# ZW with n2 innermost: contiguous 32x32 transposes, stepped copies and a stepped stationary operand

## The chip, the cores and the metric

The kernel runs on 1 core of one Trainium2 chip. The metric is device time in microseconds (us) of one execution. An execution's program uses TensorE (PE; its weight loads are listed apart as PEld), VectorE (DVE), ScalarE (ACT), GpSimd (POOL) and the DMA queues, of which SyncE's (SP) carries most loads and stores here.

## The reference

`x` has shape 8 x 3072 x 256. The first half is a convolution over the sequence by Fourier transform, the second a mixture of 8 experts with a top-1 gate and a capacity of 768 tokens per expert:

```python
X = np.fft.rfft(x, axis=1)
Y = X * (filt_r + 1j * filt_i)[None]
y = np.fft.irfft(Y, n=3072, axis=1).reshape(-1, 256)
logits = y @ w_gate                      # 256 -> 8
# token i goes to its best expert while that one has fewer than 768 tokens
h = np.maximum(einsum('ecd,edf->ecf', disp, w1), 0)     # 256 -> 1024
out = gate * einsum('ecf,efd->ecd', h, w2)              # 1024 -> 256, 0 for other tokens
```

## The kernel before

Since the experts are full after some 6144 tokens, only the first `NB0` = 3 batches (0, 1 and 2) are transformed if every expert fills up on them, which is so with these inputs. Their convolutions take the first part of the span, the experts the rest, which runs on TensorE almost without a gap.

The sequence is split as n = 32*n1 + n2 (96 x 32). For one batch and both halves `h` of 128 channels the steps are:

- `a` (L226; in batch 0 `a_half`, L217): matmuls over n1 with the table `A` as stationary operand; a bank of 512 values per partition is copied by ACT to `ZW`, a tile of 128 partitions x 2 halves x 32 (n2) x 128 (channels). One call of `a` handles 4 values of n2 in two banks, 8 calls make a batch.
- `t` (L235): four DVE instructions per batch, each of which transposes 64 of 128 channels of one half in blocks of 32 partitions x 32 values of n2, in place in `ZW`. q = 0, 1 are half 0, q = 2, 3 are half 1.
- `bm` (L239): four matmuls with `self.ZW[:, h, p, :]` (128 x 128) as stationary and the constant `Bc` as moving operand, into one bank. Each f32 matmul is two weight loads and two matmuls in the trace, so a call of `bm` is x8 there. A batch has 12 calls, 6 groups `g` by 2 halves.
- `b` (L247): DVE multiplies the bank by the filter (two instructions, L259), POOL adds and subtracts (L263, L264). `g` (L267) transposes the result back with matmuls (L276) and splits it in a high and a low part on ACT and DVE; `bi` (L283) is the inner transform back (L290), copied by ACT to `V`.
- `ti` (L335) transposes `V` as `t` does `ZW`; `V` has 144 or 128 channels innermost. `ai` (L340) is the last stage back (L349), copied by ACT to `rt` and stored by DMA.

`middle` runs `b`, `g` and `bi` in an order written out by hand: b(0,0), b(0,1), b(1,0), b(1,1), g(0), and so on; up to two steps of the `ai` of the batch before (`ahead`) are put between the first `b`s. All queues are in program order. Batch 0 computes `bm` of half 0 for all six groups right after its second half's `a_half`. For batches 1 and 2 the order is: four `ti` of the batch before, beside `a` of the new one; then the `ai` steps beside four `t`; then `middle`. In batch 2 the routing of the batch before (one-hot rows on DVE, L452 to L454, and their matmuls L462) is interleaved with these. The matmuls of L462 have operands `ol[:, :, i]` and `oh[:, :, :, i]` in f16, both with a step of 8 elements (16 bytes) between neighbours, 128 stationary columns and 96 moving ones. L430 is a DVE reduction that reads f32 with a step of 32 elements (128 bytes), L394 one of the same size that reads neighbours.

Of the kernel before, what the change touches and what calls it, by code (L numbers as in the profile page):

```python
# [9 lines left out]
F32 = mybir.dt.float32  # L10
# [6 lines left out]

# The sequence is split as n = 32*n1 + n2 (96 x 32), its frequencies as
# k = k1 + 96*k2.  Complex rows of k1 come in pairs (2 per group of 128
# partitions), a partition is (j, c, p or n2 or slot): j the member of the pair,  # L20
# c real or imaginary, p the group.
N1, N2, NP = 96, 32, 24
CH = 272  # channels of the transform back: y[0:128], 8 + 8 halves of the logits, y[128:256]
HS = ((0, 144), (144, 128))  # its two blocks: start and size

# [53 lines left out]
def fftconv_moe_kernel(ctx, tc, x, fr, fi, fny, wg, w1, w2, ca, cai, cb, out, cap):  # L79
    nc = tc.nc  # L80
    NB, SEQ, D = x.shape[0], N1 * N2, 256
    E, FF = w1.shape[0], w1.shape[2]
    NT = (cap + 127) // 128          # slot tiles of an expert
    NSLOT = E * NT                   # slot tiles in all
    NTOK = NB * SEQ
    NB0 = min(NB, -(-E * cap // SEQ) + 1)
    NF = FF // 128
    NE = min(3, NT)                  # slot tiles of the first expert that go ahead of the last batch
    assert 3 <= NB0 < NB
# [25 lines left out]
    def row_of_slot(idx, n):  # L115
        # tacc holds the token of a slot plus 1, 0 where the slot is empty
        nc.vector.tensor_scalar(out=idx, in0=tacc[:, :n], scalar1=-1.0, scalar2=0.0, op0=ALU.add, op1=ALU.max)
# [11 lines left out]
    def interleave(*lists):  # L129
        # merges the lists of steps evenly  # L130
        marks = sorted(((i + 1) / (len(l) + 1), j, i) for j, l in enumerate(lists) for i in range(len(l)))
        for _, j, i in marks:
            lists[j][i]()

    HOLD = 2  # steps of the last but one batch's transform back that run ahead of the last batch's

# [4 lines left out]
    class Conv:  # L141
        """The convolution of one batch, in steps."""

        def __init__(self, base, top, side, resident):
            self.base, self.wk, self.side, self.resident = base, top, side, resident
            self.ZW = top.tile([128, 2, N2, 128], F32, name="ZW", bufs=1)
            self.Bc = top.tile([128, 4, 128], F32, name="Bc", bufs=1)
            self.BIh = top.tile([128, 2, 128], F32R, name="BIh", bufs=1)
            self.BIl = top.tile([128, 2, 128], F32R, name="BIl", bufs=1)
            self.IG = top.tile([128, 2, 136], F32, name="IG", bufs=1)  # [1 | gate] and [gate | 1]  # L150
            self.FNY = top.tile([128, 2], F32, name="FNY", bufs=1)
            if resident:
                self.A = side.tile([N1, N2, 128], F32, name="A", bufs=1)
                self.F = [top.tile([128, 2, QS], F32, name=n, bufs=1) for n in ("FRT", "FIT")]
            self.xts, self.Fs, self.Ac, self.dropped, self.ysb, self.ycs, self.bps = {}, {}, {}, False, {}, {}, {}
# [15 lines left out]
        def drop_dc(self, t, col):  # L171
            # the transform back ignores the imaginary part of the constant term
            for h in range(2):
                nc.vector.memset(t[:, h, col:col + 1], 0.0)
# [42 lines left out]
        def a_half(self, h, c):  # L217
            xt = self.xts.pop((h, c))
            for k in range(2):
                ps = bank()  # L220
                for i in range(4):
                    nc.tensor.matmul(ps[:, i * 128:(i + 1) * 128], self.Ac[c * 2 + k][:, i, :], xt[:, k * 4 + i, :], start=True, stop=True)
                n2 = c * 8 + k * 4
                nc.scalar.copy(self.ZW[:, h, n2:n2 + 4, :], ps.rearrange("p (t d) -> p t d", d=128))  # L224

        def a(self, c):  # L226
            xt, A = self.xts.pop(c), self.Ac[c]
            for h in range(2):
                ps = bank()
                for i in range(2):  # L230
                    nc.tensor.matmul(ps[:, i * D:(i + 1) * D], A[:, h * 2 + i, :], xt[:, h * 2 + i, :], start=True, stop=True)
                n2 = c * 4 + h * 2
                nc.scalar.copy(self.ZW[:, :, n2:n2 + 2, :].rearrange("p h t d -> p t h d"), ps.rearrange("p (t h d) -> p t h d", h=2, d=128))

        def t(self, q):  # L235
            v = self.ZW[:, q // 2, :, q % 2 * 64:q % 2 * 64 + 64].rearrange("p t d -> p d t")
            nc.vector.transpose(v, v)  # L237

        def bm(self, g, h):  # L239
            ps = bank()  # L240
            for i in range(4):
                p = g * 4 + i
                nc.tensor.matmul(ps[:, i * 128:(i + 1) * 128], self.ZW[:, h, p, :],  # L243
                                 self.Bc[:, 1 if p == NP - 1 else 0, :], start=True, stop=True)
            return ps
# [48 lines left out]
        def middle(self, V, fill, first=(), last=()):  # L294
            """Steps from the transformed rows to the rows of the transform back."""
            fill, first = list(fill), list(first)
# [43 lines left out]
    def ai(V, dst, h, L=None, eng=None):  # L340
        """Steps of the last stage of the transform back, one bank of rows each."""
        c0, w = HS[h]
        k = 512 // w
# [28 lines left out]
    def route(L, last, ohp):  # L372
        """Slots of a batch's tokens: steps up to the slot, then the table of the slots' tokens."""
        t = lambda nm, sh, dt=F32: p1b.tile(sh, dt, name=nm, tag=nm, bufs=1)
# [47 lines left out]
        def f9():  # L422
            # es: 128 * NT * expert
            st["es"] = t("es", [N1, N2])
            V_.tensor_scalar(out=st["es"], in0=st["m2"][:, 0, :], scalar1=float(-128 * NT), scalar2=float(128 * NT * E),
                             op0=ALU.mult, op1=ALU.add)
# [51 lines left out]

# [1 line left out]
    W, X, Gt, H = {}, {}, {}, {}  # L480
# [8 lines left out]
    def turn(rows, n, pool, spare=False):  # L489
        """The rows' transposes in two parts; spare leaves the Vector engine alone."""  # L490
        xh = pool.tile([128, 2, n * 128], F32R, name="xh", tag="xh")
        xl = pool.tile([128, 2, n * 128], F32R, name="xl", tag="xl")
        for h in range(2):
            ps = bank()
            for i in range(n):
                nc.tensor.transpose(ps[:, i * 128:(i + 1) * 128], rows[:, i, h * 144:h * 144 + 128], ident)  # L496
            split(xh[:, h, :], xl[:, h, :], ps[:, :n * 128], pool if spare else None)
        return xh, xl
# [29 lines left out]

# [1 line left out]
    base_ctx, v_ctx, top_ctx, side_ctx, raw_ctx = (ExitStack() for _ in range(5))  # L530
# [19 lines left out]
    def routing_constants():  # L550
# [13 lines left out]
        io(nv[:, 0, :], [[1, N2]], -SEQ // 2, N2)  # L564
        # tri[p, m] = 1 where p < m
        nc.gpsimd.affine_select(out=tri, in_=ones, pattern=[[1, N1]], compare_op=ALU.is_gt, fill=0.0,
                                base=0, channel_multiplier=-1)

    def early_count():
        # reaches the capacity where the first expert's early slots are all taken  # L570
        nc.vector.tensor_tensor(out=tot[:, E:E + 1], in0=tot[:, 0:1], in1=lack, op=ALU.add)

    def full_flag():
        # the least number of tokens an expert has got, and the count of the early slots
        ps = bank()
# [7 lines left out]
    def load_w(e, raw, pool):  # L583
        """Steps that load an expert's weights and split them."""
        loads, splits, ws = [], [], []
# [22 lines left out]
    with tc.manual_schedule():  # L608
        # batches that are needed whatever the routing
        V = new_V(vp)  # L610
        order = [(h, c) for h in range(2) for c in range(4)]
        for i, (h, c) in enumerate(order):
            # the rows of V in front of its padding are free until the transform back
            dst = V[c // 3][:N1, c % 3 * 8:c % 3 * 8 + 8, 0:128] if h else None
# [10 lines left out]
        nc.vector.memset(zt, 0.0)  # L625
        # the tensor engine warms up while the first loads are under way
        ps = bank()
# [42 lines left out]

        # the last of them: its route goes on beside the last stage of the transform back
        b = NB0 - 1
# [58 lines left out]

        # the other batches only while an expert still has room
        least = nc.values_load(flag[0:1, 0:1], min_val=0, max_val=NTOK)
        with tc.If(least < cap):  # L734
            with ExitStack() as gp:
# [8 lines left out]
                with tc.For_i(NB0, NB, 1) as b:  # L744
# [14 lines left out]
                    for f in S1 + S2:  # L759
                        run(f)  # L760
                # the rows of the slots move to ybuf in slot order
                row_of_slot(idxg, NSLOT)
# [144 lines left out]
```

## Time and profile before

| | |
|---|---|
| median of 3 runs | 561.33 us (559.0 to 561.54) |
| profiled execution, span from first to last instruction | 557.8 us |
| granted TensorE clock, mean over the span | 0.945 of full |
| PE busy | 507.6 us (91%) |
| DVE, ACT, POOL busy | 315.5, 239.3, 241.5 us |
| the four stages `t` on DVE: 12 instructions | 50.3 us |

The profiled execution's own time is not listed beside its span; the runs' median lies 3.5 us above that span, the lowest run 1.2 us. Times inside the profile are counted from the first instruction. Busy times of PE overlap each other (matmuls are pipelined), so what a stretch costs is read from the starts of successive instructions.

### The profile page before, as it was taken

To read this page: it belongs to the slowest core of one execution; us is meant where nothing else is said; L and a number is where in the kernel's file an instruction comes from. 1 tells how busy PE (TensorE), PEld (TensorE's weight loads), DVE (VectorE), ACT (ScalarE), POOL (GpSimd) and SP (SyncE) were. 2 spreads that over 40 slices of the span, in tenths; PEclk is the share of its full clock that TensorE was granted. 3 is DMA by queue.
4 is the path that set the end of the run, shared out by engine and by line. 5 is a ranking of instruction groups with operands and counts; after the bars stand their busy time and mean duration, and the time that the engine had idled before them with its cause. 6 is when DMAs were issued, how large, how long until landed. Compare 5 with 4: busy or idle time off the path is not lost. (4 is left out here: it accounts for less than half of the span.)

```text
span 557.8 us, 9332 instructions
## 1 busy us (share of the span) xinstructions
PE 507.6 (91%) x3564; PEld 492.7 (88%) x3564; DVE 315.5 (57%) x531; ACT 239.3 (43%) x563; POOL 241.5 (43%) x245
## 2 busy tenths in 40 slices
PE   6789999699994998978889999999999999999992
PEld 5778989699894898976879999999999999999992
DVE  0587799787998889997134533334333353333500
ACT  3404766146640355472063633536335363363410
POOL 4016301363031650342674666836667366673021
PEclk9978999799996999888779999999999999999997
DMA  9999347990449905550430506016050160511000
GB/s 220 274 359 407 155 114 199 337 397 27 114 119 327 326 1 181 156 156 8 152 120 32 208 29 217 32 49 212 29 212 32 51 214 29 180 60 49 11 29 28
DMA packets 58420, 81.64 MB, mean 146 GB/s; under 512 B 4096, under 2 KB 37376, under 8 KB 58240
## 3 DMA queue, kind: packets, MB, share of 16 engines
q1 hardware_dynamic: 43264, 51.20, 28.9%
q10 hardware_dynamic: 10496, 16.78, 9.0%
q0 software_dynamic: 4608, 12.98, 6.5%
q8 instruction: 31, 0.51, 0.4%
q14 instruction: 21, 0.17, 0.1%
HBM read 39.46 MB, written 41.48 MB: 145 GB/s over the span
## 5 line engine op out<-in xcount | busy, mean ns | idle before, releaser
L508 DVE SCALAR_TENSOR_TENSOR hl<-ps,hh 128x384 fp32r<-128x384 f32 x124 | 67.3, 556 | 98.1 <-ACT hh L502 86.5
L826 PE MATMUL ps<-wbh,hh 128*128 128x256 f32 x384 | 109.5, 285 | 4.4 <-DVEq L734 4.4
L826 PE MATMUL ps<-wbh,hl 128*128 128x256 f32 x384 | 108.4, 282 | 0.1
L826 PE MATMUL ps<-wbl,hh 128*128 128x256 f32 x384 | 108.5, 282 | 0.0
L524 PE MATMUL ps<-xh,wah 128*128 128x384 f32 x256 | 87.8, 343 | 2.4 <-issue 1.7
L524 PE MATMUL ps<-xl,wah 128*128 128x384 f32 x256 | 87.6, 342 | 0.2 <-issue 0.2
L524 PE MATMUL ps<-xh,wal 128*128 128x384 f32 x256 | 87.4, 342 | 0.0
L830 POOL DMA_INDIRECT y<-ob,idxs x48 | 47.6, 991 | 88.7 <-ACT ob L829 85.3
L502 ACT ACTIVATE hh<-ps 128x384 fp32r<-128x384 f32 x128 | 61.7, 497 | 54.3 <-PE ps L524 48.3
L826 PEld LDWEIGHTS ps<-wbh,hh 128*128 128x128 f32 x384 | 73.6, 192 | 4.7 <-issue 4.7
L826 PEld LDWEIGHTS ps<-wbl,hh 128*128 128x128 f32 x384 | 73.7, 192 | 0.0
L826 PEld LDWEIGHTS ps<-wbh,hl 128*128 128x128 f32 x384 | 73.5, 191 | 0.2 <-issue 0.2
L263 POOL TENSOR_TENSOR t<-t,t 128x256 f32<-128x256 f32 x33 | 24.5, 742 | 86.0 <-DVE t L259 75.2
L237 DVE STREAM_TRANSPOSE ZW<-ZW 128x2048 f32<-128x2048 f32 x12 | 50.3, 4240 | 19.0 <-ACT ZW L224 19.0
L829 ACT ACTIVATE ob<-ps,gt 128x256 f32<-128x256 f32 x48 | 22.7, 472 | 89.0 <-PE ps L826 61.4
L243 PE MATMUL ps<-Bc,ZW 128*128 128x128 f32 x288 | 42.7, 307 | 16.0 <-DVE ZW L237 15.8
L485 POOL DMA_INDIRECT rows<-ybuf,idxg x45 | 45.4, 1009 | 26.9 <-DVEq L734 13.5
L243 PEld LDWEIGHTS ps<-Bc,ZW 128*128 128x128 f32 x288 | 40.4, 222 | 17.0 <-issue 16.0
L349 PE MATMUL ps<-V,AI 128*96 128x144 f32 (+1 forms) x384 | 50.9, 294 | 4.4 <-ACT rt L351 2.8
L338 DVE STREAM_TRANSPOSE V<-V 128x2304 f32<-128x2304 f32 (+1 forms) x12 | 50.7, 4260 | 5.5 <-ACT V L292 5.5
L349 PEld LDWEIGHTS ps<-V,AI 128*96 128x96 f32 x384 | 49.1, 174 | 5.3 <-ACT rt L351 3.0
L351 ACT COPY rt<-ps 96x432 f32<-96x432 f32 (+2 forms) x57 | 30.0, 541 | 52.2 <-PE ps L349 43.1
(123 smaller groups left out, 907.1 us busy)
## 6 DMA issues: line engine op xcount, KB each, us to landing
y<-zt SPq DMA_DIRECT2D x12, 2048.0 KB
raw<-w ACTq DMA_DIRECT2D x16, 1024.0 KB
xt<-x SPq DMA_DIRECT2D x16, 384.0 KB
ybuf<-rt SPq DMA_DIRECT2D x30, 162.0 KB
ybuf<-rt SPq DMA_DIRECT2D x24, 192.0 KB
A<-ca SPq DMA_DIRECT2D x8, 192.0 KB
xt<-x SPq DMA_DIRECT2D x8, 192.0 KB
V<-x SPq DMA_DIRECT2D x8, 192.0 KB
```

What stands on the lines that cost most here:

```text
L237: nc.vector.transpose(v, v)
L243: nc.tensor.matmul(ps[:, i * 128:(i + 1) * 128], self.ZW[:, h, p, :], self.Bc[:, 1 if p == NP - 1 else 0, :], start=True, stop=True)
L263: eng.tensor_tensor(out=t1[:, :, 0, :], in0=t1[:, :, 0, :], in1=t2[:, :, 1, :], op=ALU.subtract)
L338: nc.vector.transpose(v, v)
L349: nc.tensor.matmul(ps[:N1, i * w:(i + 1) * w], AI[:, n0 + i, :], V[h][:, n0 + i, :], start=True, stop=True)
L351: nc.scalar.copy(rt[:, :n * w], ps[:N1, :n * w])
L485: nc.gpsimd.indirect_dma_start(out=rows[:, t, :], out_offset=None, in_=yrows[:lim, :], in_offset=bass.IndirectOffsetOnAxis(ap=idx[:, j + t ...
L502: nc.scalar.activation(out=hi, in_=ps, func=f)
L508: nc.vector.scalar_tensor_tensor(out=lo, in0=ps, scalar=0.0, in1=hi.bitcast(F32), op0=ALU.max, op1=ALU.subtract)
L524: nc.tensor.matmul(ps[:, :n * 128], w[:, kk, m * 128:(m + 1) * 128], y[:, kk, o], start=k == 0, stop=k == 5)
L826: nc.tensor.matmul(ps[:, :D], y[:, m, o], w[:, m, :], start=m == 0 and j == 0, stop=m == NF - 1 and j == 2)
L830: ins = nc.gpsimd.indirect_dma_start(out=out, out_offset=bass.IndirectOffsetOnAxis(ap=idxs[:, j:j + 1], axis=0), in_=ob, in_offset=None, b ...
```

## The change

`ZW` becomes 128 partitions x 2 halves x 128 channels x 32 (n2). The four transposes of a batch then read and write 2048 neighbouring values of a partition in order. The copies out of PSUM write 4 neighbouring values, then step 128 bytes; to do so they read the bank with a step of 128 values (512 bytes). `a` is cut so that one bank holds one half and four values of n2, as `a_half` had it: 4 matmuls of 128 moving columns for a bank in place of 2 of 256. The stationary operand of `bm` has a step of 32 values (128 bytes) between its columns.

```diff
-            self.ZW = top.tile([128, 2, N2, 128], F32, name="ZW", bufs=1)
+            self.ZW = top.tile([128, 2, 128, N2], F32, name="ZW", bufs=1)
...
-                nc.scalar.copy(self.ZW[:, h, n2:n2 + 4, :], ps.rearrange("p (t d) -> p t d", d=128))
+                nc.scalar.copy(self.ZW[:, h, :, n2:n2 + 4], ps.rearrange("p (t d) -> p d t", d=128))
...
-                for i in range(2):
-                    nc.tensor.matmul(ps[:, i * D:(i + 1) * D], A[:, h * 2 + i, :], xt[:, h * 2 + i, :], start=True, stop=True)
-                n2 = c * 4 + h * 2
-                nc.scalar.copy(self.ZW[:, :, n2:n2 + 2, :].rearrange("p h t d -> p t h d"), ps.rearrange("p (t h d) -> p t h d", h=2, d=128))
+                for i in range(4):
+                    nc.tensor.matmul(ps[:, i * 128:(i + 1) * 128], A[:, i, :], xt[:, i, h * 128:(h + 1) * 128], start=True, stop=True)
+                nc.scalar.copy(self.ZW[:, h, :, c * 4:c * 4 + 4], ps.rearrange("p (t d) -> p d t", d=128))
...
-            v = self.ZW[:, q // 2, :, q % 2 * 64:q % 2 * 64 + 64].rearrange("p t d -> p d t")
+            v = self.ZW[:, q // 2, q % 2 * 64:q % 2 * 64 + 64, :]
             nc.vector.transpose(v, v)
...
-                nc.tensor.matmul(ps[:, i * 128:(i + 1) * 128], self.ZW[:, h, p, :],
+                nc.tensor.matmul(ps[:, i * 128:(i + 1) * 128], self.ZW[:, h, :, p],
```

## Rows read from the trace of the kernel before

**Rows 1.** First line of the page.

```profile
span 557.8 us, 9332 instructions
```

**Rows 2.** Waits of PE, 0 to 214 us: total us, times, longest.

```profile
PE ps L243 <- DVE ZW L237: 15.8, 4, 7.5
...
PE ps L276 <- POOL t L264: 2.0, 4, 0.8
...
PE pr L408 <- DVE cs L404: 1.2, 2, 0.8
```

**Rows 3.** Timeline of DVE, batch 0 to 1: start us, us, instruction.

```profile
69.33 16.43 DVE L338 STREAM_TRANSPOSE V<-V 128x2304 f32<-128x2304 f32 x4 [2.59 <-ACT V L292]
85.68 16.55 DVE L237 STREAM_TRANSPOSE ZW<-ZW 128x2048 f32<-128x2048 f32 x4
```

**Rows 4.** Timeline of PE, batch 0 to 1.

```profile
68.82 13.98 PE L231 MATMUL ps<-xt,A 96*128 96x256 f32 x64
...
95.72 1.06 PE L243 MATMUL ps<-Bc,ZW 128*128 128x128 f32 x8
102.37 2.05 PE L243 MATMUL ps<-Bc,ZW 128*128 128x128 f32 x8 [5.60 <-DVE ZW L237]
...
108.31 1.06 PE L243 MATMUL ps<-Bc,ZW 128*128 128x128 f32 x8
...
138.41 8.80 PE L231 MATMUL ps<-xt,A 96*128 96x256 f32 x40
```

**Rows 5.** Timeline of PE, batch 0.

```profile
28.66 7.18 PE L243 MATMUL ps<-Bc,ZW 128*128 128x128 f32 x48
38.04 3.20 PE L243 MATMUL ps<-Bc,ZW 128*128 128x128 f32 x16 [2.19 <-DVE ZW L237]
...
44.54 1.65 PE L243 MATMUL ps<-Bc,ZW 128*128 128x128 f32 x8
```

**Rows 6.** Timelines of DVE and of PE, batch 1 to 2.

```profile
173.00 4.14 DVE L237 STREAM_TRANSPOSE ZW<-ZW 128x2048 f32<-128x2048 f32 x1
...
168.62 1.13 PE L243 MATMUL ps<-Bc,ZW 128*128 128x128 f32 x8 [0.47 <-DVE ZW L237]
177.28 2.05 PE L243 MATMUL ps<-Bc,ZW 128*128 128x128 f32 x8 [7.54 <-DVE ZW L237]
...
183.33 1.56 PE L276 MATMUL ps<-IG,t 128*128 128x136 f32 x12
```

**Rows 7.** DVE's groups of instructions, shapes apart, 0 to 270 us: busy, mean ns.

```profile
L237 DVE STREAM_TRANSPOSE ZW<-ZW 128x2048 f32<-128x2048 f32 x12 | 50.3, 4240 | 19.0 <-ACT ZW L224 19.0
L280 DVE TENSOR_TENSOR yl<-ps,yh 128x408 fp32r<-128x408 f32 x48 | 26.5, 575 | 5.9 <-ACT yh L279 4.6
...
L338 DVE STREAM_TRANSPOSE V<-V 128x2304 f32<-128x2304 f32 x6 | 25.0, 4194 | 5.5 <-ACT V L292 5.5
...
L430 DVE TENSOR_REDUCE s<-cs 96x32 f32<-96x256 f32 x3 | 1.8, 603 | 0.0
...
L394 DVE TENSOR_REDUCE m<-sc 96x32 f32<-96x256 f32 x3 | 1.2, 416 | 0.1
```

**Rows 8.** Timeline of PE's weight loads at two places.

```profile
110.48 1.87 PEld L243 LDWEIGHTS ps<-Bc,ZW 128*128 128x128 f32 x16
112.27 1.46 PEld L276 LDWEIGHTS ps<-IG,t 128*128 128x128 f32 x12
...
155.72 1.31 PEld L462 LDWEIGHTS <-ol 96*128 96x128 f16 x8
157.07 3.05 PEld L349 LDWEIGHTS ps<-V,AI 128*96 128x96 f32 x24
```

**Rows 9.** Instructions on tile ZW: ns min/median/max, first and last start.

```profile
L233 ACT COPY ZW<-ps x32: 586/586/590, 69.9 to 153.8; 128x512 f32<-128x512 f32 x32
```

**Rows 10.** Windows of batch 1's middle: length, busy by engine, granted clock, DMA.

```profile
102.40:109.20 6.80, 6.80 (x40) 6.80 (x41) 3.82 (x7) 1.16 (x2) 2.81 (x4) 0.65 1.04 383
109.20:138.40 29.20, 28.44 (x238) 27.87 (x237) 24.84 (x53) 16.11 (x61) 15.92 (x22) 1.00 0.62 235
```

## The prediction

> **What bounds the kernel now.** I read the list of PE's waits first, then the timelines of PE and DVE around each wait, then the groups by duration. The span is 557.8 us [rows 1], the median 561.33, so 3.5 us lie outside the span; the sum is made on the span and added to the median. Every step of the change lies before 214 us. After that the experts run in an order that no edit touches, so a delay or gain before 214 us moves the end by as much. Up to there the reader is to see one large wait [rows 2]: PE waits 15.8 us, in four pieces, for the transposes of `ZW`; the next causes are 2.0 us (POOL) and 1.2 us (the routing's scan). So PE is the bound nearly everywhere, and DVE only where a batch's eight transposes stand in a row.
>
> The three places: in batch 0 PE has done half 0's six `bm` calls (x48) and waits 2.19 us until 38.04 [rows 5]. Between batches 0 and 1 DVE works without a break from 69.33, four `ti` and then four `t` of 16.55 us together [rows 3]; PE finishes `ai` and bm(0,0) at 96.8 and waits until 102.37, 5.60 us [rows 4]. Between batches 1 and 2 it waits 7.54 us until 177.28 [rows 6]. [...]
>
> **The transposes.** Twelve at 4.24 us each [rows 7]. What does contiguous access make of them? `V`'s transposes move 2304 values in 4.19 us, less time than 2048 values of `ZW` take [rows 7]; the step between values is 576 bytes there and 512 here. So the time goes by the access pattern, not only by the count. Two reductions of 256 values differ in their step alone: 603 ns with 128 bytes (L430), 416 ns without (L394) [rows 7], so a step costs (603 - 416)/256 = 0.73 ns per value. Without a step the rate is (575 - 416)/(408 - 256) = 1.05 ns per value (L280 against L394), by which 2048 values take 0.416 + 1792 x 1.05 ns = 2.3 us. Bounds: 2.3 to 4.24 us (nothing gained). I take 2.3, since the stepped reduction comes to 1.05 + 0.73 = 1.78 ns per value, close to the transpose's 4240/2048 = 2.07. A batch's four save 7.8 us of DVE.
>
> **A's copies.** Now 586 ns for 512 values [rows 9]. No row has a stepped read of PSUM or a stepped write of ACT. Below: nothing, 0.59 us. Above: DVE's 0.73 ns per value, once for the read, once more for the write, 0.59 + 0.37 + 0.37 = 1.33 us. I take one of the two, 0.96, since the write keeps runs of four. That is hidden: the first copy starts at 69.9 [rows 9], sixteen at 0.96 end at 85.3, and `t` does not start before 85.68, behind `ti` [rows 3]. The cover is gone from (85.68 - 69.9)/16 = 0.99 us on.
>
> **A's matmuls.** 64 matmuls of 256 columns take 13.98 us [rows 4]; now they are 128 of 128 columns, each with a weight load. A pair of this size starts every (112.27 - 110.48)/16 = 0.112 us [rows 8], so 14.3 us: +0.4 us in batches 1 and 2.
>
> **B's stationary operand.** This decides. A weight load of 128 columns and its matmul take 0.112 us now, 0.9 us per call of `bm`. The only matmuls with stepped operands are L462's, and they start every (157.07 - 155.72)/8 = 0.169 us [rows 8], although they are f16 and stream only 96 columns. If the moving operand set that pace, it took 0.169/96 = 1.76 ns per stepped value, DVE's 1.78 again; a load of 128 stepped columns at this rate takes 0.22 us and can no longer hide behind its matmul. If the stationary operand set it, a stepped column costs 0.169/128 = 1.32 ns, and a pair of `bm` 0.169 us. If neither carries over to f32, 0.112 us stays. Bounds: 0.112 to 0.225 us a pair. I take 0.22, because two engines agree on that price for a value that is read with a step. Then a `bm` call takes 1.76 us, 0.86 us more, and PE, the bound, pays this.
>
> [...]
>
> **The sum, place by place.** Batch 0: from 28.66 to 41.24 PE runs 64 pairs and the wait [rows 5]; 64 x 0.22 us end at 42.7, so +1.5, and the wait is swallowed. The 3.3 us up to bm(2,1) at 44.54 ran at the low clock (8 pairs in 1.65 us there); without idle time before them I take 0.9 us back. Three later calls cost 0.86 each, +2.6; bm(2,1) itself +0.1; of the small waits on ACT and POOL 0.7 us disappear behind the slower PE. Together +2.6.
>
> Batch 1: `t` ends at 85.7 + 4 x 2.3 = 94.9, so PE no longer waits. It reaches bm(0,0) at 95.72 + 0.4 = 96.1; four `bm` calls and two `ai` steps between them (8 pairs, 0.9 us each) end at 96.1 + 7.0 + 1.8 = 104.9, against 109.2 (108.31 and 0.9) [rows 4]: -4.3. The other eight calls cost +6.9, of which the 0.8 us of waits on POOL and the scan in this middle absorb as much. Together +1.8.
>
> Batch 2: DVE's last transpose ends at 177.1 - 7.8 = 169.3 [rows 6]. PE starts bm(0,0) at 168.2 + 0.4 = 168.6 (its wait of 0.47 goes); four calls and one `ai` step end at 168.6 + 7.0 + 0.9 = 176.5, against 183.33 [rows 6]: -6.8. Then +6.9, less about 1.5 of the 2.0 us of waits there. Together -1.4.
>
> Sum: +2.6 + 1.8 - 1.4 = +3.0 us: 560.8 us of span, 561.33 + 3.0 = 564.3 us by the median. The 15.8 us of waiting, and the low clock behind it, are traded for 36 slower `bm` calls. A measurement of this kernel tells about 0.5% (2.8 us) from no change, so this is slower by barely that much.
>
> **Rivals.** *The stationary operand takes its step for free* (pairs stay at 0.112 us). For it: L462's loads read 128 stepped columns in 0.169 us at most, so that stream is not at 1.76 ns there. Against it: they are f16, with a 16-byte step. Batch 0 gains the wait and the low clock, 3.0; batch 1 has four `bm` and two `ai` from 96.1 to 101.5, 7.7 earlier; in batch 2 bm(0,1) starts at 169.4 and bm(1,1) ends at 173.0, 10.3 earlier. Together -21.0: 540.3 us, faster. Between it and the forecast lies the pair of 0.169 us (1.35 us a call): -2, -3.1 and -6.3, 550 us. The sign turns at about 0.21 us a pair.
>
> [...]
>
> *ACT becomes late.* With both prices, 1.33 us a copy, batch 1's last copy ends at 69.9 + 21.3 = 91.2, the last transpose at about 99, and the `ai` copies queue behind on ACT and hold PE's banks. I count 2.5 us in batch 1 and 2 in batch 2 on top of the forecast: 569 us. It decides from 0.99 us a copy on.
>
> *The transposes do not get faster* (the block order, not the memory, sets 2 ns per value). Then the waits stay, and 0.86 us is paid on each call outside them and outside the low clock: about +2.6, +7 and +6.5: 577 us. `V`'s 4.19 us for more values speaks against it.
>
> **Numbers.** Chances: forecast 0.52 (559 to 570 with 0.20 to 0.225 us a pair and 2.3 to 2.6 us a transpose), free stationary operand 0.21, the pair in between 0.12, ACT late 0.09, transposes unchanged 0.06. The range 539 to 571 leaves out the last case and the tails. Faster: 0.21 + 0.12 + 0.05 of the forecast's = 0.38; same (558.5 to 564.1): 0.23 of the forecast's; slower: 0.24 + 0.09 + 0.06 = 0.39. The forecast's own part sits astride the bound, so the three are near each other; 564 stands because it is the likeliest single case.
>
> **What would show it.** In the profile after: the mean of L237 (2.3 us expected); the mean of A's copies on ACT (0.96); the distance between starts of L243's weight loads in a run of eight (0.22); PE's wait for `ZW` gone from the list; the granted clock near 1.00 behind bm(0,0) of batches 1 and 2. Wrong it is if L243's pairs still start every 0.11 us (then 540), or if L237 stays at 4.2. What I can't bound: whether slower pairs, which leave PE's array idle for half of each, let the granted clock fall in batch 0's run of 64; that would cost some more us.

## The result, and the profile after

Measured side by side, the kernel after takes 564.8 us (median of 20 runs, 561.57 to 568.32), the kernel before 562.62 us (20 runs, 556.42 to 565.79): a ratio of 1.0053 with an interval of 1.0029 to 1.0078. (The ratio is not the quotient of the two medians, which is 1.0039.) The forecast was 564 us (564.3 by its sum), or +3.0 us. The profiled execution took 562.22 us with a span of 560.4 us, 2.6 us above that of before [rows 1].

First the page of the kernel after: span and busy times.

```profile
span 560.4 us, 9588 instructions
...
PE 529.5 (94%) x3692; PEld 520.4 (93%) x3692; DVE 294.3 (53%) x531; ACT 238.7 (43%) x563; POOL 240.6 (43%) x245
```

DVE's busy time fell by 21.2 us and PE's rose by 21.9 us. The edit removes one line, so `bm` is now L242, `t` L236 and the copy of `a` L232. The view of the tile `ZW` in the kernel after (ns min/median/max, first and last start):

```profile
L242 PEld LDWEIGHTS ps<-Bc,ZW x288: 292/313/333, 28.8 to 207.0; 128*128 128x128 f32 x144
...
L232 ACT COPY ZW<-ps x32: 585/585/585, 74.2 to 159.9; 128x512 f32<-128x512 f32 x32
...
L236 DVE STREAM_TRANSPOSE ZW<-ZW x12: 2256/2284/2334, 18.3 to 172.8; 128x2048 f32<-128x2048 f32 x12
```

A transpose takes 2.28 us instead of 4.24 [rows 7]; A's copies take 585 ns as before [rows 9]. Next the weight loads of batch 1's middle in the kernel after, which answer to [rows 8]:

```profile
110.72 3.60 PEld L242 LDWEIGHTS ps<-Bc,ZW 128*128 128x128 f32 x16
114.23 1.48 PEld L275 LDWEIGHTS ps<-IG,t 128*128 128x128 f32 x12
```

Sixteen loads, from 110.72 to 114.23, make 0.219 us for a pair of load and matmul, against 0.112. The waits of PE up to 214 us in the kernel after (total us, times, longest), against [rows 2]:

```profile
PE ps L222 <- DMA V<-x: 3.6, 1, 3.6
PE ps L628 <- DVE zt L624: 1.5, 1, 1.5
PE ps L275 <- POOL t L263: 0.8, 1, 0.8
```

No wait for `ZW` is left. Who waits instead stands in the list of DVE's waits, same stretch, first of the kernel after and then of the kernel before:

```profile
DVE t L258 <- PE ps L242: 24.4, 22, 5.9
```

```profile
DVE t L259 <- PE ps L243: 8.3, 8, 2.0
```

DVE waits 24.4 us for the banks of `bm`; before it was 8.3. The idle time has moved from PE to DVE, and in its place PE is occupied with slower loads. Now PE's timeline of the kernel after, place by place, against [rows 4 to 6]:

```profile
29.04 14.14 PE L242 MATMUL ps<-Bc,ZW 128*128 128x128 f32 x64
43.03 0.47 PE L275 MATMUL ps<-IG,t 128*128 128x136 f32 x2
44.28 1.43 PE L275 MATMUL ps<-IG,t 128*128 128x136 f32 x10 [0.79 <-POOL t L263]
45.86 1.99 PE L242 MATMUL ps<-Bc,ZW 128*128 128x128 f32 x8
...
73.07 14.68 PE L231 MATMUL ps<-xt,A 96*128 96x128 f32 x128
87.58 13.25 PE L348 MATMUL ps<-V,AI 128*96 128x144 f32 x112
...
109.45 1.56 PE L275 MATMUL ps<-IG,t 128*128 128x136 f32 x12
...
144.04 9.09 PE L231 MATMUL ps<-xt,A 96*128 96x128 f32 x80
...
181.50 1.56 PE L275 MATMUL ps<-IG,t 128*128 128x136 f32 x12
...
216.07 4.53 PE L348 MATMUL ps<-V,AI 128*96 128x128 f32 x40
```

Two of these, 43.03 and 216.07, answer to these rows of PE's timeline in the kernel before:

```profile
41.02 0.66 PE L276 MATMUL ps<-IG,t 128*128 128x136 f32 x2
...
213.86 4.53 PE L349 MATMUL ps<-V,AI 128*96 128x128 f32 x40
```

So the kernel after is 4.25 us late when `a` of batch 1 starts (73.07 against 68.82), 5.63 us at `a` of batch 2 (144.04 against 138.41) and 2.21 us at 216. The windows of the kernel after over the two parts of batch 1's middle (length, busy by engine, granted clock, DMA) answer to [rows 10]:

```profile
100.70:109.40 8.70, 8.70 (x50) 8.70 (x49) 4.61 (x8) 1.75 (x3) 3.44 (x5) 1.00 1.00 258
109.40:144.00 34.60, 34.60 (x237) 34.60 (x238) 25.07 (x51) 16.03 (x61) 15.18 (x22) 1.00 0.68 256
```

The granted clock is 1.00 where it was 0.65 on average behind the wait (0.50 from 102.37 to 105.50, 0.77 from there to 109.20 in the kernel before), and PE is busy in the whole of both windows.

### The profile page after: what moved, and what is told of

Same layout as the page of the kernel before. It is cut to its first block, busy times and chain, and to the rows that moved or that the text cites. A ratio compares the mean times of both kernels' runs of the same rounds, so it can differ in the third digit from the quotient of the medians.

```text
span 560.4 us, 9588 instructions
## 1 busy us (share of the span) xinstructions
PE 529.5 (94%) x3692; PEld 520.4 (93%) x3692; DVE 294.3 (53%) x531; ACT 238.7 (43%) x563; POOL 240.6 (43%) x245
## 5 line engine op out<-in xcount | busy, mean ns | idle before, releaser
L242 PE MATMUL ps<-Bc,ZW 128*128 128x128 f32 x288 | 66.4, 385 | 0.3 <-ACT V L291 0.2
L242 PEld LDWEIGHTS ps<-Bc,ZW 128*128 128x128 f32 x288 | 64.7, 312 | 0.7 <-ACT V L291 0.4
L262 POOL TENSOR_TENSOR t<-t,t 128x256 f32<-128x256 f32 x33 | 24.4, 738 | 83.3 <-DVE t L258 70.7
L348 PE MATMUL ps<-V,AI 128*96 128x144 f32 (+1 forms) x384 | 49.0, 287 | 3.5 <-ACT rt L350 1.9
L278 ACT CAST yh<-ps 128x408 fp32r<-128x408 f32 x48 | 24.0, 499 | 66.2 <-PE ps L275 60.7
L523 PEld LDWEIGHTS ps<-xh,wah 128*128 128x128 f32 x256 | 48.7, 190 | 3.6 <-issue 2.5
L348 PEld LDWEIGHTS ps<-V,AI 128*96 128x96 f32 x384 | 47.2, 168 | 4.2 <-ACT rt L350 2.1
```

The lines of the kernel that those rows point to most:

```text
L262: eng.tensor_tensor(out=t1[:, :, 0, :], in0=t1[:, :, 0, :], in1=t2[:, :, 1, :], op=ALU.subtract)
L278: nc.scalar.copy(fh[:, o], ps[:, :408])
L348: nc.tensor.matmul(ps[:N1, i * w:(i + 1) * w], AI[:, n0 + i, :], V[h][:, n0 + i, :], start=True, stop=True)
L523: nc.tensor.matmul(ps[:, :n * 128], w[:, kk, m * 128:(m + 1) * 128], y[:, kk, o], start=k == 0, stop=k == 5)
```

## The experiments

The theory: the change is two edits of opposite sign that happen to cancel: the step that DVE's transposes lose (4.24 us each, now 2.28) is now in PE's weight loads (0.112 us a pair, now 0.219). The rivals are that something else holds PE, and that it is a step as such, or its size, that costs. The kernel before was run again beside each group of experiments (558.81 us with the first four, 554.2 us with the last two), so ratios are compared and not times.

**1. The change without the step on PE.** The stationary operand is a run of 128 neighbouring values of the same tile. The output is then not the convolution. The second edit keeps the branch to further batches closed, so that wrong expert choices can't add work.

```diff
-                nc.tensor.matmul(ps[:, i * 128:(i + 1) * 128], self.ZW[:, h, :, p],
+                w = self.ZW[:, h].rearrange("p a b -> p (a b)")[:, 1924 + 4 * p:2052 + 4 * p]
+                nc.tensor.matmul(ps[:, i * 128:(i + 1) * 128], w,
...
-        with tc.If(least < cap):
+        with tc.If(least < 0):
```

> The changed kernel, but B's stationary operand is 128 neighbouring values of ZW (a stand-in that overlaps both transposes of its half, so the output is not the convolution; the branch to further batches is kept closed). Theory (the step of the stationary operand alone eats the transposes' gain): pairs of weight load and matmul back at 0.112 us, transposes at 2.3 us, no wait for ZW, 541 to 545 us. Rival (the loss comes from another part of the change, the cut matmuls of A or the copies): about 563 us, as the changed kernel.

Measured: 535.4 us, ratio 0.961 (0.9532 to 0.9688). The tile `ZW` in this kernel:

```profile
L243 PEld LDWEIGHTS ps<-Bc,ZW x288: 186/192/333, 28.1 to 181.6; 128*128 128x128 f32 x144
...
L236 DVE STREAM_TRANSPOSE ZW<-ZW x12: 2256/2264/2312, 18.1 to 155.0; 128x2048 f32<-128x2048 f32 x12
```

The loads are back at their old duration (192 ns at the median here and in the kernel before, 313 in the changed kernel), the transposes stay fast, and of PE's wait for `ZW` 0.7 us remains. The time lies below the 541 to 545 us that were expected; on the 562.62 us of the main comparison the ratio makes 540.7 us. From this kernel to the changed one, each by its ratio to the kernel before, is 1.0053/0.961 = 1.046: the step on PE alone eats a gain of 3.9%. The cut matmuls and the stepped copies are in this kernel too, so they are not what eats it.

**2. The step on PE without the change.** In the kernel before, the stationary operand gets the same step of 32 values; here too the branch is closed as in experiment 1.

```diff
-                nc.tensor.matmul(ps[:, i * 128:(i + 1) * 128], self.ZW[:, h, p, :],
+                w = self.ZW[:, h].rearrange("p a b -> p (a b)").rearrange("p (k s) -> p k s", s=32)[:, :, p]
+                nc.tensor.matmul(ps[:, i * 128:(i + 1) * 128], w,
```

> The kernel before (ZW with channels innermost, transposes with a step of 512 bytes), but B's stationary operand is read with a step of 32 values (a stand-in, so the output is not the convolution; the branch to further batches is kept closed). Theory: pairs at 0.22 us wherever the clock is high, transposes still 4.24 us, PE's waits for ZW still there, and about half of the slower calls hidden in them: 577 us (573 to 581). Rival (the two prices simply add): 562.6 + 36 calls at 0.86 us = 593 us; or nothing (562) if the step costs only in the new layout.

Measured: 573.92 us, ratio 1.027 (1.0206 to 1.0335). Its weight loads at one place in batch 1:

```profile
117.20 3.60 PEld L244 LDWEIGHTS ps<-Bc,ZW 128*128 128x128 f32 x16
120.70 1.48 PEld L277 LDWEIGHTS ps<-IG,t 128*128 128x128 f32 x12
```

A pair takes (120.70 - 117.20)/16 = 0.219 us. PE's wait for `ZW` in this kernel, up to 225 us:

```profile
PE ps L244 <- DVE ZW L237: 11.9, 3, 6.5
```

And the first call of `bm` behind the wait of batch 1, in PE's timeline:

```profile
107.82 2.09 PE L244 MATMUL ps<-Bc,ZW 128*128 128x128 f32 x8 [4.91 <-DVE ZW L237]
```

The two edits don't add up: -3.9% and +2.7% make -1.2%, and together they give +0.5%. The same step costs 4.6% where the transposes are fast and 2.7% where they are slow, since beside slow transposes part of it lies in time that PE would lose anyway. The wait fell from 15.8 us to 11.9. And behind the wait the eight instructions take 2.09 us, hardly more than the 2.05 us that they took there without the step [rows 4]; the granted clock is 0.50 in both (the eight matmuls of `ai` behind them take 1.71 us in both, from 109.70 to 111.41 and from 104.21 to 105.92), and there a pair takes 0.23 us with the step or without it. Summed over the starts of PE's instructions and without the waits, `bm` costs 24.3 us more here than in the kernel before, and 29.2 us more in the changed kernel than in experiment 1.

**3. Which step costs what.** The changed kernel with a step of 1, 2, 3, 4, 8 or 32 values for groups 0 to 5 (a single run; branch closed as in experiment 1). Its time of 555.48 us mixes the six steps and is not used.

```diff
+                s = (1, 2, 3, 4, 8, 32)[g]
+                o = 0 if s == 32 else 1924
+                w = self.ZW[:, h].rearrange("p a b -> p (a b)")[:, o:o + 128 * s].rearrange("p (k s) -> p k s", s=s)[:, :, 0]
+                nc.tensor.matmul(ps[:, i * 128:(i + 1) * 128], w,
```

A line, here and below, is 16 neighbouring bytes of a partition, which is four f32 values. To count by that size was the author's assumption, and this run tests it.

> The changed kernel with stand-ins for B's stationary operand: a step of 1, 2, 3, 4, 8 and 32 values in groups 0 to 5 (output is not the convolution; the branch to further batches is kept closed). Distance of starts in runs of eight pairs. Theory (the price is for each 16-byte line that gives fewer than two values): 0.112 us at steps 1 and 2, something between at 3, 0.22 us at 4, 8 and 32. Rival 1 (any step costs): 0.22 from 2 on. Rival 2 (it grows with the step): 32 well above 4.

Measured, in the timeline of weight loads of batch 1's middle; the distance from a row of L245 to the row behind it is the time of its 16 or 8 pairs:

```profile
99.46 1.86 PEld L245 LDWEIGHTS ps<-Bc,ZW 128*128 128x128 f32 x16
101.24 0.93 PEld L351 LDWEIGHTS ps<-V,AI 128*96 128x96 f32 x8
102.12 1.02 PEld L245 LDWEIGHTS ps<-Bc,ZW 128*128 128x128 f32 x8
103.06 0.93 PEld L351 LDWEIGHTS ps<-V,AI 128*96 128x96 f32 x8
...
106.26 2.85 PEld L245 LDWEIGHTS ps<-Bc,ZW 128*128 128x128 f32 x16
109.02 1.47 PEld L278 LDWEIGHTS ps<-IG,t 128*128 128x128 f32 x12
...
111.92 3.81 PEld L245 LDWEIGHTS ps<-Bc,ZW 128*128 128x128 f32 x16
115.64 1.48 PEld L278 LDWEIGHTS ps<-IG,t 128*128 128x128 f32 x12
...
120.69 3.89 PEld L245 LDWEIGHTS ps<-Bc,ZW 128*128 128x128 f32 x16
124.49 1.48 PEld L278 LDWEIGHTS ps<-IG,t 128*128 128x128 f32 x12
...
127.02 3.60 PEld L245 LDWEIGHTS ps<-Bc,ZW 128*128 128x128 f32 x16
130.53 1.48 PEld L278 LDWEIGHTS ps<-IG,t 128*128 128x128 f32 x12
```

| step, values | 16-byte lines under 128 columns | us a pair |
|---|---|---|
| 1 | 32 | 1.78/16 = 0.111 |
| 2 | 64 | 0.94/8 = 0.118 |
| 3 | 96 | 2.76/16 = 0.173 |
| 4 | 128 | 3.72/16 = 0.233 |
| 8 | 128 | 3.80/16 = 0.238 |
| 32 | 128 | 3.51/16 = 0.219 |

The granted clock is 1.00 in all six stretches, and batch 2's middle repeats steps 2 to 32 to within 0.001 us a pair. The time goes by the number of lines: 1.7 to 1.9 ns each from 96 lines on, and up to 64 lines it hardly shows (0.118 us against 0.111). That a step as such costs is refuted by step 2, that the cost grows with the step by step 32. Why steps 4 and 8 are 6 to 8% dearer than 32 stays open.

That 16 bytes is the size to count by rests on these rows: from step 2 to step 4 a pair goes from 0.118 us to 0.233, and from step 4 to 8 and 32 it grows no more (0.238 and 0.219), though lines of 32 bytes would be twice as many at 8 as at 4. What in the hardware makes it so is not shown.

**4. Two neighbours on each line, for both engines.** With two values on each line a pair of experiment 3 took 0.118 us (step 2). A layout in which pairs of n2 are innermost gives DVE's transposes and PE's loads two values per line; that this serves DVE too was an assumption, which this run tests. The whole computation is done.

```diff
-            self.ZW = top.tile([128, 2, 128, N2], F32, name="ZW", bufs=1)
+            self.ZW = top.tile([128, 2, N2 // 2, 128, 2], F32, name="ZW", bufs=1)
...
-                nc.scalar.copy(self.ZW[:, h, :, c * 4:c * 4 + 4], ps.rearrange("p (t d) -> p d t", d=128))
+                nc.scalar.copy(self.ZW[:, h, c * 2:c * 2 + 2], ps.rearrange("p (k j d) -> p k d j", j=2, d=128))
...
-            v = self.ZW[:, q // 2, q % 2 * 64:q % 2 * 64 + 64, :]
+            v = self.ZW[:, q // 2, :, q % 2 * 64:q % 2 * 64 + 64, :].rearrange("p k d j -> p d k j")
...
-                nc.tensor.matmul(ps[:, i * 128:(i + 1) * 128], self.ZW[:, h, :, p],
+                nc.tensor.matmul(ps[:, i * 128:(i + 1) * 128], self.ZW[:, h, p // 2, :, p % 2],
```

> A version that computes the reference: ZW with pairs of n2 innermost, 16 x 128 channels x 2. The stationary operand has a step of 2 values (8 bytes), the transposes read and write two neighbours and then step 1024 bytes. Theory (two values a line are enough on both engines): pairs at 0.112 us, transposes near 2.3 us, 541 to 545 us. Rival (only fully contiguous access is fast): pairs at 0.22 and transposes at 3.3 to 4.2, 570 to 577 us; if two values a line serve one engine alone, 550 to 565 us.

Measured: 543.94 us, ratio 0.9711 (0.9633 to 0.9789). The tile `ZW` in this kernel:

```profile
L242 PEld LDWEIGHTS ps<-Bc,ZW x288: 193/196/333, 30.1 to 185.0; 128*128 128x128 f32 x144
...
L236 DVE STREAM_TRANSPOSE ZW<-ZW x12: 2257/2305/2316, 18.4 to 158.0; 128x2048 f32<-128x2048 f32 x12
```

Both engines are near their fast time: 2.31 us a transpose, and loads of 196 ns at the median against 313 in the changed kernel; a pair takes 0.118 us, as step 2 did. This version beats both kernels; the changed layout took the right access for DVE and one too coarse for PE.

**5. The same for `V`.** `V`'s transposes still had their step (4.2 to 4.3 us each). `V` in pairs too, on top of experiment 4; the whole computation is done.

```diff
-                    nc.scalar.copy(v[:, p, :], ps[:, c0:c0 + n])
+                    nc.scalar.copy(v[:, p // 2, :, p % 2], ps[:, c0:c0 + n])
...
-        v = V[q // 2][:, :, q % 2 * n:(q % 2 + 1) * n].rearrange("p t d -> p d t")
+        v = V[q // 2][:, :, q % 2 * n:(q % 2 + 1) * n, :].rearrange("p k d j -> p d k j")
...
-                nc.tensor.matmul(ps[:N1, i * w:(i + 1) * w], AI[:, n0 + i, :], V[h][:, n0 + i, :], start=True, stop=True)
+                nc.tensor.matmul(ps[:N1, i * w:(i + 1) * w], AI[:, n0 + i, :], V[h][:, (n0 + i) // 2, :, (n0 + i) % 2], start=True, stop=True)
...
-        return [pool.tile([128, N2, n], F32, name=f"V{c}") for c, n in HS]
+        return [pool.tile([128, N2 // 2, n, 2], F32, name=f"V{c}") for c, n in HS]
...
```

> A version that computes the reference: ZW and V both with pairs of n2 innermost, so that V's transposes read and write two neighbours too, ACT writes V with a step of 8 bytes, and the last stage's moving operand has a step of 8 bytes. Theory (two values of a line are enough for a moving f32 operand as well): V's transposes fall from 4.29 to about 2.4 us, L349's pairs stay at 0.118 us, and with DVE no longer late in the last batch 3 to 8 us less than with pairs in ZW alone: ratio to the kernel before 0.957 to 0.966. Rival (a moving operand pays for any step): L349's 384 pairs at 0.2 us or more, 20 to 30 us lost, ratio above 1.

Measured: 533.55 us against 554.2, ratio 0.9637 (0.9607 to 0.9668). DVE's groups by shape in this kernel (busy us, mean ns):

```profile
L337 DVE STREAM_TRANSPOSE V<-V 128x2304 f32<-128x2304 f32 x6 | 15.2, 2563 | 5.5 <-ACT V L291 5.5
L337 DVE STREAM_TRANSPOSE V<-V 128x2048 f32<-128x2048 f32 x6 | 13.7, 2292 | 0.0
```

`V`'s transposes fall to 2.56 and 2.29 us. The matmuls that read `V` with a step of two values as moving operand nearly keep their pace, as their weight loads show:

```profile
79.55 13.66 PEld L348 LDWEIGHTS ps<-V,AI 128*96 128x96 f32 x112
93.16 1.96 PEld L242 LDWEIGHTS ps<-Bc,ZW 128*128 128x128 f32 x16
```

112 of them start over 13.61 us, 0.122 us each; in the kernel after the same 112 take 0.117. PE waits for no transpose any more, though still 4.5 us for the routing's scan on DVE (L403) up to 250 us. That this beats experiment 4 is not shown: 0.7% lies between the two ratios, and their intervals overlap.

**6. Which operand set L462's pace.** The prediction took 0.22 us from reading L462's 0.169 us as the cost of its stepped moving operand. Here the four chunks of a batch's table have different layouts of the two operands: chunk 0 a contiguous stationary one, chunk 1 a contiguous moving one, chunk 2 both, chunk 3 as before (a single run; the whole computation is done).

```diff
-            ol = ohp.tile([N1, 128, 8], F16, name="ol", tag="ol")
-            oh = ohp.tile([N1, 2, NSLOT, 8], F16, name="ohh", tag="ohh")
+            ol = ohp.tile([N1, 1024], F16, name="ol", tag="ol")
+            ol = ol.rearrange("p (i l) -> p l i", i=8) if c in (0, 2) else ol.rearrange("p (l i) -> p l i", i=8)
+            oh = ohp.tile([N1, 16 * NSLOT], F16, name="ohh", tag="ohh")
+            oh = oh.rearrange("p (i a s) -> p a s i", i=8, a=2) if c in (1, 2) else oh.rearrange("p (a s i) -> p a s i", i=8, a=2)
```

> The changed kernel; the operands of the table's matmuls (L462 of the kernel before) are laid out so that in chunk 0 the stationary, in chunk 1 the moving, in chunk 2 both are contiguous, and chunk 3 is as it was; DVE writes them with a step instead. It computes the reference. Theory (the prediction's reading: the moving operand sets the 0.169 us): chunks 0 and 3 stay near 0.17 us a pair, chunks 1 and 2 fall below 0.12. Rival (the stationary operand sets it, at 1.32 ns a column): chunks 0 and 2 fall, chunk 1 stays.

Measured, in the timeline of weight loads in chunk order; the matmul is L463 here:

```profile
154.42 1.31 PEld L463 LDWEIGHTS <-ol 96*128 96x128 f16 x8 [0.76 <-DVE ol L454]
155.79 8.63 PEld L231 LDWEIGHTS ps<-xt,A 96*128 96x128 f32 x48
...
166.54 0.64 PEld L463 LDWEIGHTS <-ol 96*128 96x128 f16 x8
167.07 2.96 PEld L348 LDWEIGHTS ps<-V,AI 128*96 128x96 f32 x24
...
175.09 0.58 PEld L463 LDWEIGHTS <-ol 96*128 96x128 f16 x7 [1.81 <-issue]
175.61 4.15 PEld L348 LDWEIGHTS ps<-V,AI 128*96 128x96 f32 x18
181.54 1.47 PEld L463 LDWEIGHTS <-ol 96*128 96x128 f16 x8 [1.78 <-DVE ol L454]
183.05 3.90 PEld L348 LDWEIGHTS ps<-V,AI 128*96 128x96 f32 x20
```

With the step on the moving operand alone a pair takes (155.79 - 154.42)/8 = 0.171 us, on the stationary one alone 0.53/8 = 0.066, on neither 0.52/7 = 0.074, on both 1.51/8 = 0.189. The 0.074 was taken at a granted clock of 0.50, the others at 0.96 to 1.00; and the 0.189 holds a wait of the first matmul, which starts at 181.81 (from there it is (183.22 - 181.81)/8 = 0.176). So the moving operand sets the pace, as the prediction read it. Its price does not follow TensorE's clock: with the step on both operands in the next table, at a clock of 0.50, eight matmuls take from 254.85 to 256.25 us, 0.175 each. The kernel took 594.83 us, for a reason of its own, which stands in the last section.

## Why the prediction was right

**The transposes** were put at 2.3 us, at a rate read from two unlike instructions of the same engine (L280, a subtraction, and L394, a reduction); they take 2.28. That the rate of those would be the transpose's was assumed. PE's waits for `ZW` are gone, and the granted clock behind bm(0,0) is 1.00, as said.

**B's stationary operand** was the deciding term, taken at 0.22 us a pair; it takes 0.219. Experiments 3 and 6 bear out the price, with lines in place of stepped values: 1.7 to 1.9 ns for each 16-byte line, on the moving side of L462 (0.171 us over 96 lines) and in f32 weight loads (0.173 us over 96, 0.219 to 0.238 over 128) alike. But the step from an f16 moving operand to an f32 stationary one rested on no row: L462's own stationary operand has the same 16-byte step and pays nothing that shows (0.066 us a pair), as the first rival suspected. That it came out is in part luck, and that DVE's price for a stepped value has the same cause as PE's is not shown. The rival that stationary operands take their step for free was right about f16 (0.066 us) and wrong about f32. Its arithmetic held: it gave 540.3/561.33 = 0.963, and experiment 1, which makes its condition true, measures 0.961. The rival of unchanged transposes gave 577/561.33 = 1.028, and experiment 2, which has slow transposes beside the step but not the cut matmuls, measures 1.027.

**A's copies** are the term that was mis-sized: 0.96 us forecast, 0.585 measured. That had no effect, because the copies were hidden either way; for the same reason the rival of a late ACT (from 0.99 us a copy on) did not arise.

**The sum** of +3.0 us meets the span's +2.6, but its parts are off by up to 2 us. Nor was it a firm call: faster, same and slower had been given 0.38, 0.23 and 0.39.

| | forecast | measured, in lateness of PE |
|---|---|---|
| batch 0 | +2.6 | +4.25 |
| batch 1 | +1.8 | 5.63 - 4.25 = +1.4 |
| batch 2 | -1.4 | 2.21 - 5.63 = -3.4 |
| sum | +3.0 | +2.2 |

The table counts to 216 us; 0.4 us of the span's +2.6 come later. In batch 0 four small items are missing, by the starts of PE's instructions. The stage starts 0.4 us later (29.04 against 28.66 [rows 5]), which the sum did not touch. The stretch from the end of those 64 pairs to bm(2,1) takes 45.86 - 43.03 = 2.83 us instead of 44.54 - 41.02 = 3.52 (the prediction's 3.3 us count from the modelled end of those pairs), so 0.7 came back and not 0.9: the clock there rose from 0.50 to 1.00, but the wait for POOL grew from 0.4 us to 0.8. bm(2,1) costs 0.3 us more (1.83 against 1.49) and not 0.1. And the 0.7 us of small waits on POOL and ACT did not go; 0.79 us of it stands in the timeline above. The fear that PE's array, idle for half of each slow pair, would pull the clock down was not borne out there: the window from 29.04 to 45.86 has a clock of 0.94, against 0.71 in the same stretch before.

In batch 1, A's cut matmuls cost 0.7 us (87.58 - 73.07 = 14.51 us against 82.64 - 68.82 = 13.82) and not 0.4; bm(1,1) ends at 109.45, 4.0 us earlier relative to the start of `a` (forecast 4.3), and the rest takes 34.6 us against 29.2 [rows 10], +5.4 where +6.1 was forecast.

In batch 2 the part up to bm(1,1) gains 7.5 us (forecast 6.8; 181.50 against 183.33 [rows 6], with 5.63 us of lateness made up), and the rest costs +4.0 where +5.4 was forecast. In both rests the eight calls themselves cost the +6.9 of the sum. What is off lies beside them: all 2.0 us of batch 2's small waits went, and not 1.5, and the matmuls between the calls take 0.8 us less there and 0.7 us less in batch 1, for a reason that stays open. So PE lost more than assumed in batch 0 and less in batches 1 and 2; that these nearly cancel is luck.

## What to carry to other kernels

A layout change moves a step from one engine to another, so price it on each engine that reads or writes the tile, and ask which of them is the bound once the wait is gone: here a busy-time gain of 21 us on DVE bought nothing, because PE paid as much. Count the 16-byte lines that an f32 stationary operand or a moving operand touches, not the step: here each line cost 1.7 to 1.9 ns from 96 lines on, while 64 lines left an f32 pair at 0.118 us (an f16 stationary operand did not pay here, 0.066 us a pair). Where two engines want opposite orders, try two f32 neighbours innermost: here that served both (2.31 us a transpose, 0.118 us a pair). The same cost is worth less where it can lie in a wait (2.7%) than where the wait has been removed (4.6%), so effects of two edits measured alone should not be added.

## What was unexpected of the hardware

- ACT does not mind: its copy of 512 values takes 585 to 586 ns whether it reads PSUM contiguously or with a step of 512 bytes, and whether it writes 512-byte or 16-byte runs.
- An f16 stationary operand with a step of 16 bytes costs nothing that shows: a pair of 128 columns takes 0.066 us at a clock of 1.00, where an f32 one with a step of 16 bytes takes 0.233 us. A contiguous f16 one was measured at a clock of 0.50 alone (0.074 us). Why f16 pays nothing where f32 does is not shown.
- In experiment 6 DVE's comparison of 1024 f16 values took 4.78 us where it writes them with a step of 256 bytes, against 0.80 us in order. The rows of `oh`, which it writes with a step in chunks 1 and 2, pay likewise (the first of them 2.10 and 2.20 us, against 0.37 and 0.43 in chunks 0 and 3). Before these matmuls, the last of which starts at 304.0 us, PE sits idle 27.5 us for DVE's rows, in a span that is 32.6 us longer than that of the kernel after (593.0 against 560.4). Two rows of `ol` in the timeline of DVE, chunk 0 and chunk 3:

```profile
149.59 4.78 DVE L454 TENSOR_TENSOR ol<-iol,lof 96x1024 f16<-96x1024 f16 x1
...
180.69 0.80 DVE L454 TENSOR_TENSOR ol<-iol,lof 96x1024 f16<-96x1024 f16 x1
```
